# Stored weight sets loaded by quarters, sums reordered, and side work moved in a fused attention and feed-forward kernel

## The chip, the cores and the metric

The kernel runs on one core of a Trainium2 chip. TensorE (PE) multiplies into PSUM; VectorE (DVE) and ScalarE (ACT) read PSUM, convert, add and copy; GpSimd (POOL) does a little; SyncE (SP) issues nearly all the DMAs, from one queue in order. Each engine works through its own queue in order. The metric is the time of one execution on the device in microseconds.

## The reference

```python
scores = 30 * tanh((q @ k.T / 8) / 30)          # 4 batches x 12 heads, 448 x 448, head size 64
attn   = exp(scores - max) / (sum + 1e-9) @ v
x  = attn, heads side by side                    # 1792 tokens x 768
h  = ((x @ w1) * (x @ w2)) @ w3 @ w_out          # 768 -> 1024 -> 1024 -> 768
h  = h @ w_in                                    # 768 -> 1024
s  = h * softmax(h)                              # over 1024
ln = (s - mean(s)) / sqrt(var(s) + 1e-6) * g_ln
out = ln @ moe2_w_out                            # 1024 -> 768
```

## The kernel before

All numbers are float32, and every product is made of float32r matmuls of a high and a low part: three matmuls (high x high, high x low, low x high) for one. A "split" is a cast to the high part on ScalarE or VectorE and a subtraction on VectorE for the low part.

**Attention and fold.** Scores, `tanh`, `exp` and the products with `v` run pair of heads by pair of heads. Between them PE folds `w3 @ w_out @ w_in` into one matrix `w_dr` (DRAM) and starts the gated products. The order is made while the program is built, by a planner (`Order`, `Ahead`) that gives each step a due time from written-out costs. `Ahead` holds a list of tasks (a load into one of three `ld` buffers, a conversion on VectorE, a cast); `plan_w(f)` converts block `f` of `w1` and `w2`, `plan_last(f)` scales block `f` of the output weights by `g_ln` and stores it in `wg_dr`, `plan_x` normalizes the attention's result. A task is loaded and begun in the order of the list.

**Gated products** (`ab`, L1097). Token groups (passes) 0 and 1 are multiplied with all eight blocks of `w1` and `w2`, passes 2 and 3 with two of them, in the plain way. When the attention is over (near 365 us) the rest of the list is emitted two tasks for every 18 matmuls (`fill`, `ahead.step(2)`), and Tile's scheduler orders each engine's queue. In that rest are: `t` sums (`plan_sums("t")`, four subtractions over pieces of `w_dr`, through four `ts` buffers to `tw_dr`), `tg` sums (the same over `wg_dr`, to `tg_dr`), `T` and `U` (sums of the activations, `two_three` and `one_four`), the first weight set and its sums (`first_set`), and the blocks `ws[1]` and `ws[2]` of the folded matrix (`plan_block`), of which `ws[2]` lies in memory that the `U` sums read.

**Seven-product blocks** (`multiply`, L1309). For passes 2 and 3 and the other six blocks n = 0 to 5, seven products of half size stand in for eight: ORDER is 1, 2, 6, 7, 5, 4, 3. Products 1, 2, 7 and 4 take stored weights, 5, 6 and 3 sums of them (`combine`, `combine_low`, `high12`, `low12`). Products 1, 6, 5 and 3 accumulate in one bank `u`, 7 and 4 in a bank `v`; after product index j, `finish(n, j)` copies the bank (`p1s`, `u2s`, `p7s`, ScalarE L1313) or adds it to such a copy (VectorE L1316), and the next product into that bank waits for it. `side[(n, j)]` holds work that is emitted between product j and its `finish`, so that it stands ahead of it in every queue. The weights of set n come from `w12_dr`, and sets n and n + 2 share a place.

**Gated stage** (r = 0 to 6, L1420). Seven products per round with the folded matrix `ws[m]`, then softmax, norm, and rounds 7 to 13 with `wg[m]` in the same way. In round 0 the blocks `ws[5]`, `ws[4]` and `ws[3]` are still being split (`high_w`, ScalarE; `low_w`, VectorE) by `side` entries.

```python
for n in range(AGAIN):
    for j in range(len(ORDER)):
        multiply(n, j)
        for todo in side.pop((n, j), ()):
            todo()
        finish(n, j)
```

Of the kernel before, what the change touches and what calls it, by code (L numbers as in the profile page):

```python
# [241 lines left out]
def attention_moe_solu(ctx: ExitStack, tc: tile.TileContext, q, k, v, cap, w12, w3t, wo, win, wout2, g_ln, out):  # L242
# [422 lines left out]
    plan_o((1, 1))  # L665
    plan_3(0, 6, 7)
    plan_o((2, 0), (3, 0), (2, 1), (3, 1), (4, 0), (4, 1), (5, 0), (5, 1))
    for f in range(3):
        plan_last(f)
    plan_3(1, *range(NF))  # L670
    for f in range(3, 6):
        plan_last(f)
    for c in range(NC):
        plan64(("i", 0, c), win[c, 0], HALF, lambda key=("i", 0, c): slot3(key), reached(passed(1, c - 1) if c else STAGE1 // 2))
    for c in range(NC):
# [258 lines left out]
    plan_w(0)
    plan_x(0)
    plan_w(1)
    plan_x(1)
    for f in range(2, NF):
        plan_w(f)
        if f >= 6:  # L940
            plan_last(f)
    plan_x(2)
    plan_x(3)
    sets, tx, AGAIN = {}, {}, NF - 2
    QUARTER = DM // 2
    AT = {1: (0, 0), 2: (0, 1), 7: (0, 2), 4: (0, 3), 5: (1, 0), 6: (1, 1), 3: (1, 2)}

    def part12(n, m):
        t, at_ = AT[m]
        return sets[n][t][:, :, at_ * QUARTER:(at_ + 1) * QUARTER]  # L950

    def load_set(n):

        if n % 2 == 0:
            sets[n] = [place["set"].tile([P, 2, w * QUARTER], F32R, tag=f"set{w}", name=f"q{w}_{n}") for w in (4, 3)]
        else:
            sets[n] = [res[0].tile([P, 2, 2 * DM], F32R, tag="wres", bufs=2, name=f"q4_{n}")]
        for half in (slice(2 * QUARTER, None), slice(0, 2 * QUARTER)):
            sync.dma_start(out=raw(sets[n][0][:, :, half]), in_=w12_dr[n][:, :, half])

    def set_more(n):
        sets[n].append(res[0].tile([P, 2, 2 * DM], F32R, tag="wres", bufs=2, name=f"q3_{n}"))

    def pieces(n, m):
        t = part12(n, m)
# [18 lines left out]
    def combine_low(n, m):  # L984
        t = whole[n, m]
        b, op_ = (whole.pop((n, m, 0)), ALU.add) if m in (5, 7) else (pieces(n, 1)[1], ALU.subtract) if m == 6 else (pieces(n, 2)[1], ALU.add)
        dve.tensor_tensor(t, t, b, op_)

    def high12(n, m):
        act.copy(part12(n, m)[:, 0], whole[n, m])  # L990
# [3 lines left out]
        dve.tensor_tensor(t[:, 1], whole.pop((n, m)), raw(t[:, 0]), ALU.subtract)  # L994

    def first_set():
        for m in (5, 7, 6):
            combine(0, m)
            combine_low(0, m)
            high12(0, m)  # L1000
        combine(0, 3)
        combine_low(0, 3)
# [11 lines left out]
    def plan_plain(key, do, test, load=lambda: None):  # L1014
        ahead.add(key, load, list, lambda: [("none", 0, 0, 0, do)], None, since(test))
# [13 lines left out]
    def one_four(c):  # L1029
# [10 lines left out]
        dve.tensor_tensor(t, t, l, ALU.add)  # L1040
        split(t4[:, 0], t4[:, 1], t)

    plan_plain("set0", lambda: None, lambda: "set" in place, lambda: load_set(0))
    for i_ in range(NF // 2):
        for part in range(2):
            plan_sums("t", W4, tw_dr, i_, part, HALF // 2)
    for c in range(NC // 2):
        plan_plain(("T", c), lambda c=c: two_three(c), lambda: (NF - 1, 0) in fin)
    for part in range(2):
        plan_block(EARLY[0], part)  # L1050
    for c in range(NC // 2):
        plan_plain(("U", c), lambda c=c: one_four(c), lambda: (NF - 1, 1) in fin)
    plan_plain("first set", first_set, lambda: "set" in place)
    for part in range(2):
        plan_block(EARLY[1], part)
    EARLY_G = 4
    for i_, part in [(i_, part) for i_ in range(NF // 2) for part in range(2)][:EARLY_G]:
        plan_sums("tg", G4, tg_dr, i_, part, DM // 4)
    plan_plain("set1", lambda: None, lambda: (NF, PASSES[1][1]) in fin, lambda: load_set(1))

    def gated_tile(t):
# [5 lines left out]

    begun = {}

    def first_operands():  # L1070
        x1, x2 = lands["x0"], lands["x1"]
        s1, s2 = first_sums = [conv.tile([P, HALF], U32, tag="cv", bufs=2, name=f"s{i}_0").bitcast(F32) for i in (1, 2)]
        begun["sums"] = first_sums

        def begin(m, x):
            begun[m] = w3p.tile([P, 2, HALF], F32R, tag="w3", bufs=W3, name=f"a0_{m}")
            split(begun[m][:, 0], begun[m][:, 1], x)
        begin(1, x1[:, :HALF])
        begin(2, x1[:, HALF:])
        dve.tensor_tensor(s1, x2[:, :HALF], x2[:, HALF:], ALU.add)  # L1080
        dve.tensor_tensor(s2, s1, x1[:, :HALF], ALU.subtract)
        begin(6, s2)
    def gated():
        pp = {}

# [200 lines left out]
        pass  # L1286
    while ahead.step(1):
        pass
    set_more(1)

    side, pu, keeps = {}, {}, {}
    LATER = AGAIN - 1
# [28 lines left out]
    def finish(n, j):  # L1321
        if j in (0, 2, 3):
            keep12(n, *{0: ("u", "p1"), 2: ("u", "u2"), 3: ("v", "p7")}[j])
        elif j == 1:
            plus("y", "p1")
        elif j == 4:
            plus("u", "p7")
        elif j == 5:
            plus("v", "u2")
            dve.tensor_tensor(keeps["u2"], keeps["u2"], keeps["p1"], ALU.mult)  # L1330
            given(n, PASSES[1][0], "u2")
        else:
            dve.tensor_tensor(keeps["p7"], pu["u"], keeps["p7"], ALU.mult)
            given(n, PASSES[1][1], "p7")
# [21 lines left out]
    sums_of = {}

    def tg_load(k):
        landing(f"tg{k}", four(G4, *divmod(k, 2), DM // 4), DM, F32)
        sums_of[k] = []  # L1360

    def tg_half(k, m):
        summed(f"tg{k}", tg_dr, *divmod(k, 2), DM // 4, m, sums_of[k])

    for n in range(AGAIN):
        plan(n, 0, (low12, n, 6), (low12, n, 7), (high12, n, 3))
        plan(n, 1, (low12, n, 5))
        plan(n, 2, (low12, n, 3))
        if n + 1 < AGAIN:
            plan(n, 2, (combine, n + 1, 5))  # L1370
            plan(n, 3, (combine_low, n + 1, 5), (combine, n + 1, 7))
            plan(n, 4, (combine_low, n + 1, 7), (combine, n + 1, 6))
            plan(n, 5, (combine_low, n + 1, 6), (high12, n + 1, 7))
            plan(n, 6, (combine, n + 1, 3), (combine_low, n + 1, 3), (high12, n + 1, 6), (high12, n + 1, 5))
        if n + 2 < AGAIN:
            plan(n, 6, (load_set, n + 2))
            if n % 2:
                plan(n + 1, 0, (set_more, n + 2))
        if n < 2 * NF // 2 - EARLY_G:
            plan(n, 0, (tg_load, EARLY_G + n))  # L1380
            plan(n, 3, (tg_half, EARLY_G + n, 0))
            plan(n, 4, (tg_half, EARLY_G + n, 1))
    plan(LATER - 1, 0, (load_first,))
    plan(LATER, 0, (last_sets,), (load_ws, EARLY[2]), (load_ws, EARLY[3]))
    plan(LATER, 3, (first_operands,))
    plan(LATER, 5, (high_w, ws, EARLY[2], 0), (low_w, ws, EARLY[2], 0))
    plan(LATER, 6, (high_w, ws, EARLY[2], 1), (low_w, ws, EARLY[2], 1), (high_w, ws, EARLY[3], 0))
    with tc.manual_schedule():
# [343 lines left out]
```

## Time and profile before

| | us |
|---|---|
| runs shown: median (lowest to highest) | 794.2 (793.58 to 794.28) |
| profiled execution | 795.62 |
| its span, first to last instruction | 793.8 |
| PE busy in the span | 773.2 |
| VectorE, ScalarE busy | 615.9, 442.2 |

The stages lie in the span so: attention and fold to 365, gated products 270 to 458, six seven-product blocks 458.4 to 550.7, rounds of the gated stage and of the output after that. Times in the rows are from the start of the span. "Busy" counts an instruction from its start to its end; "idle before" is what an engine waited ahead of it, and the releaser is the instruction or DMA whose end let it go.

### The profile page before, as it was taken

Reading aid. Unit: us, or ns where it says so; the run is one execution under the profiler, and the core shown is the slowest. Engines: PE = TensorE matmul, PEld = TensorE weight load, DVE = VectorE, ACT = ScalarE, POOL = GpSimd, SP = SyncE. Lnnn points to the kernel's source line nnn. Section 1 sums busy time; section 2 is a strip of 40 time slices with the busy share of each in tenths; the row PEclk is TensorE's granted clock in tenths of the full one; section 3 lists DMA queues with packets and bytes.
Section 4 is the critical chain, followed back from the end, with each engine's and each line's share of the span. In section 5 each row is a group of like instructions: output and inputs, shape, how many; then the busy total and the mean of one; then the engine's idle time right before and its main releaser. Section 6 shows DMA issues by size and latency. Waiting matters only on the chain.

```text
span 793.8 us, 11282 instructions
## 1 busy us (share of the span) xinstructions
PE 773.2 (97%) x3956; PEld 611.9 (77%) x3956; DVE 615.9 (78%) x1129; ACT 442.2 (56%) x659; POOL 55.1 (7%) x106
## 2 busy tenths in 40 slices
PE   9999999999999999999999959999999999999998
PEld 6556665776866776777999958888688888899998
DVE  6997898989974578865788858787786668878973
ACT  6787867447477766762332212224576666845642
POOL 0111100001010121100000000000011111100000
PEclk9999999999999999999999979999999999999999
DMA  8767868777872484727867884665743335996432
GB/s 282 250 227 235 274 216 293 248 261 247 297 213 79 132 271 142 285 76 294 299 226 251 257 293 165 216 223 173 245 141 123 108 95 132 273 196 134 140 93 80
DMA packets 147672, 162.45 MB, mean 205 GB/s; under 512 B 66148, under 2 KB 116512, under 8 KB 146592
## 3 DMA queue, kind: packets, MB, share of 16 engines
q1 hardware_dynamic: 144880, 155.91, 61.1%
q0 software_dynamic: 2592, 5.73, 3.0%
q8 instruction: 31, 0.51, 0.3%
q14 instruction: 25, 0.20, 0.1%
q10 hardware_dynamic: 144, 0.10, 0.0%
HBM read 114.04 MB, written 47.53 MB: 204 GB/s over the span
## 4 chain that ended last, share of the span: by engine, by line
PE 71%; DMA 11%; DVE 9%; ACT 5%; issue 3%; SPq 1%; DVEq 0%; ACTq 0%
PE u L1420 14%; PE o L523 9%; PE f L775 8%; PE v L1420 7%; PE ab L1097 7%; PE f L759 6%; PE sc L442 6%; PE y L1420 4%; PE us L1309 3%; DMA ldtg<-wg_dr 2%; PE n L523 2%; PE sc L438 2%; DMA ws<-w_dr 2%; DMA wg_dr<-wg 1%; PE vs L1309 1%
## 5 line engine op out<-in xcount | busy, mean ns | idle before, releaser
L1097 PE MATMUL ab<-xs,wt 128*128 128x448 f32 x720 | 148.0, 364 | 0.0
L1097 PEld LDWEIGHTS ab<-xs,wt 128*128 128x128 f32 x720 | 134.3, 188 | 14.4 <-issue 5.2
L455 ACT ACTIVATE sc<-sc,small 128x896 f32<-128x896 f32 (+1 forms) x96 | 82.8, 887 | 46.2 <-PE sc L442 41.4
L460 ACT ACTIVATE p<-sc,small 128x896 f32<-128x896 f32 (+1 forms) x96 | 84.8, 921 | 0.6
L1420 PE MATMUL u<-ws,a 128*128 128x512 f32 x336 | 80.6, 391 | 1.8 <-ACT u L1424 1.3
L523 PE MATMUL o<-p,vd 128*64 128x448 f32 x384 | 77.5, 545 | 0.0
L1420 PEld LDWEIGHTS u<-ws,a 128*128 128x128 f32 x336 | 62.8, 188 | 16.1 <-ACT u L1424 1.8
L759 PE MATMUL f<-w,w_o 128*128 128x512 f32 x288 | 70.8, 396 | 0.0
L775 PE MATMUL f<-w_i,w 128*128 128x512 f32 x288 | 68.6, 393 | 0.0
L759 PEld LDWEIGHTS f<-w,w_o 128*128 128x128 f32 x288 | 53.2, 188 | 16.4 <-issue 3.4
L775 PEld LDWEIGHTS f<-w_i,w 128*128 128x128 f32 x288 | 53.4, 188 | 14.5 <-issue 3.0
L1420 PE MATMUL u<-wg,a 128*128 128x384 f32 x336 | 62.1, 335 | 0.0
L1420 PEld LDWEIGHTS u<-wg,a 128*128 128x128 f32 x336 | 58.5, 188 | 0.5 <-DVE a L1551 0.2
L523 PEld LDWEIGHTS o<-p,vd 128*64 128x64 f32 x384 | 25.4, 136 | 41.2 <-issue 39.9
L331 DVE SCALAR_TENSOR_TENSOR cv<-ld,cv 128x512 uint32<-128x512 uint32 (+1 forms) x80 | 51.7, 659 | 0.8
L334 DVE SCALAR_TENSOR_TENSOR cv<-ld,cv 128x512 uint32<-128x512 uint32 (+1 forms) x80 | 51.8, 660 | 0.7
L1547 ACT CAST a<-s 128x512 fp32r<-128x512 f32 (+1 forms) x42 | 31.3, 754 | 33.4 <-DVE s L1569 16.3
L1551 DVE TENSOR_TENSOR a<-s,a 128x512 fp32r<-128x512 f32 (+1 forms) x42 | 35.5, 852 | 10.2 <-ACT a L1547 10.1
L1420 PE MATMUL v<-ws,a 128*128 128x512 f32 x168 | 40.4, 389 | 0.0
L328 DVE TENSOR_SCALAR cv<-ld 128x512 uint32<-128x512 uint32 (+1 forms) x80 | 32.0, 405 | 10.1 <-ACT wg L652 4.2
L1420 PEld LDWEIGHTS v<-ws,a 128*128 128x128 f32 x168 | 31.5, 188 | 6.6
L481 DVE TENSOR_TENSOR s<-p,p 128x896 f32<-128x896 f32 x18 | 19.6, 1090 | 21.3 <-PE n L523 17.0
(190 smaller groups left out, 1306.2 us busy)
## 6 DMA issues: line engine op xcount, KB each, us to landing
ld<-in_w SPq DMA_DIRECT2D x24, 512.0 KB, 4.9
w_dr<-wt SPq DMA_DIRECT2D x6, 1536.0 KB, 7.8
q<-w_dr SPq DMA_DIRECT2D x12, 768.0 KB, 6.7
ld<-in_w3t SPq DMA_DIRECT2D x16, 512.0 KB, 4.6
w_dr<-e SPq DMA_DIRECT2D x28, 256.0 KB, 3.4
ldx<-ab_dr SPq DMA_DIRECT2D x14, 512.0 KB, 4.3
c_dr<-h SPq DMA_DIRECT2D x14, 512.0 KB, 2.7
ldx<-c_dr SPq DMA_DIRECT2D x56, 128.0 KB, 3.3
```

Of the source, the lines that this page charges most:

```text
L328: dve.tensor_scalar(d[1], d[0][:, :, 1], 5, 2, ALU.logical_shift_left, ALU.logical_shift_right)
L331: dve.scalar_tensor_tensor(d[1], d[0][:, :, 1], 0xC0000000, d[1], ALU.bitwise_and, ALU.bitwise_or)
L334: dve.scalar_tensor_tensor(d[1], d[0][:, :, 0], 29, d[1], ALU.logical_shift_right, ALU.bitwise_or)
L442: pe.matmul(sc[:, j, :S], keys[rows], qq[rows, :], start=(m == 0), stop=(m == len(terms) - 1))
L455: act.activation(sc[:, :w, :S], sc[:, :w, :S], AF.Tanh, scale=qscale)
L460: act.activation(p, sc[:, :w, :S], AF.Exp, scale=capt)
L523: pe.matmul(dst[i * width:(i + 1) * width, :S], weights, moving, start=first, stop=stop)
L759: pe.matmul(banks_[c][0], lw[:, a], fw["3", h, g][:, e], start=begins, stop=(g == NF - 1 and m == 2))
L775: pe.matmul(begun_[m_][0], w34[m_][:, a, c, :], rw[:, e], start=(c == 0 and m == 0), stop=(c == NC - 1 and m == 2))
L1097: pe.matmul(pp[f, b, i][0][:, :S], w[:, u], xs[b, c][:, e], start=begins, stop=(c == NC - 1 and m == 2))
L1420: pe.matmul(banks[g], a[r][m][:, p, k * P:(k + 1) * P], b[m][:, e, k, :], start=(first and k == 0 and i == 0), stop=(k == NF // 2 - 1 and ...
L1551: dve.tensor_tensor(lo, source(r, m), raw(hi), ALU.subtract)
```

## The change

Three parts. **Sets.** A set is no longer loaded as two halves in the last product of a block, but as four quarters in products 1, 2, 4 and 6, each into the place that the block's own products have left; each quarter is now contiguous in a partition. The `tg` sums leave the blocks' side work. **Sums.** The sums of the next set are made in the order 7, 5, 6, 3 (before 5, 7, 6, 3), the last low sum slips into the next block, the low parts of a set are all made in its first two products, and the store of `u2s` goes out one product later. **Order elsewhere.** In the task list, `plan_last(0)` to `(5)` move from among the fold's weights to behind `w(0)`, `w(1)` and `w(5)`; `t` sums stand between `w(5)`, `w(6)` and `w(7)`; `first_set` and then four `tg` sums stand ahead of `T`, the other four ahead of `U`. In block 5 the split of the sixth operand moves from product index 3 to 4, and in round 0 the splits of `ws[5]`, `ws[4]`, `ws[3]` move to later products.

```diff
@@ plan of the fold's weights @@
-    for f in range(3):
-        plan_last(f)
     plan_3(1, *range(NF))
-    for f in range(3, 6):
-        plan_last(f)
@@ task list of the gated products @@
...
-    for f in range(2, NF):
-        plan_w(f)
-        if f >= 6:
-            plan_last(f)
-    plan_x(2)
-    plan_x(3)
...
+    plan_w(0)
+    plan_x(0)
+    for f in range(3):
+        plan_last(f)
+    plan_w(1)
+    plan_x(1)
+    for f in range(3, 5):
+        plan_last(f)
+    for f in range(2, 6):
+        plan_w(f)
+    plan_x(2)
+    plan_x(3)
+    plan_last(5)
     plan_plain("set0", lambda: None, lambda: "set" in place, lambda: load_set(0))
-    for i_ in range(NF // 2):
-        for part in range(2):
-            plan_sums("t", W4, tw_dr, i_, part, HALF // 2)
+    plan_t(0, 1)
+    plan_w(6)
+    plan_last(6)
+    plan_t(2, 3, 4)
+    plan_w(7)
+    plan_last(7)
+    plan_t(5, 6, 7)
+    plan_plain("first set", first_set, lambda: "set" in place and ("x", B - 1, NPAIR // 2 - 1) in xq.done)
+    plan_tg(0, 1, 2, 3)
     for c in range(NC // 2):
         plan_plain(("T", c), lambda c=c: two_three(c), lambda: (NF - 1, 0) in fin)
     for part in range(2):
         plan_block(EARLY[0], part)
+    plan_tg(4, 5, 6, 7)
     for c in range(NC // 2):
         plan_plain(("U", c), lambda c=c: one_four(c), lambda: (NF - 1, 1) in fin)
-    plan_plain("first set", first_set, lambda: "set" in place)
     for part in range(2):
         plan_block(EARLY[1], part)
-    EARLY_G = 4
-    for i_, part in [(i_, part) for i_ in range(NF // 2) for part in range(2)][:EARLY_G]:
-        plan_sums("tg", G4, tg_dr, i_, part, DM // 4)
     plan_plain("set1", lambda: None, lambda: (NF, PASSES[1][1]) in fin, lambda: load_set(1))
@@ sets @@
     def load_set(n):
...
-        for half in (slice(2 * QUARTER, None), slice(0, 2 * QUARTER)):
-            sync.dma_start(out=raw(sets[n][0][:, :, half]), in_=w12_dr[n][:, :, half])
+        open_set(n, 0)
+        if n == 0:
+            open_set(n, 1)
+        for q in (0, 2, 3, 1):
+            load_quarter(n, q)
+    def load_quarter(n, q):
+        sync.dma_start(out=raw(sets[n % 2, 0][:, q]), in_=w12_dr[n][:, :, q * QUARTER:(q + 1) * QUARTER])
     def first_set():
-        for m in (5, 7, 6):
+        for m in (7, 5, 6):
             combine(0, m)
             combine_low(0, m)
+        for m in (7, 5, 6):
             high12(0, m)
@@ side work of the blocks @@
     for n in range(AGAIN):
-        plan(n, 0, (low12, n, 6), (low12, n, 7), (high12, n, 3))
-        plan(n, 1, (low12, n, 5))
-        plan(n, 2, (low12, n, 3))
-        if n + 1 < AGAIN:
-            plan(n, 2, (combine, n + 1, 5))
-            plan(n, 3, (combine_low, n + 1, 5), (combine, n + 1, 7))
-            plan(n, 4, (combine_low, n + 1, 7), (combine, n + 1, 6))
-            plan(n, 5, (combine_low, n + 1, 6), (high12, n + 1, 7))
-            plan(n, 6, (combine, n + 1, 3), (combine_low, n + 1, 3), (high12, n + 1, 6), (high12, n + 1, 5))
-        if n + 2 < AGAIN:
-            plan(n, 6, (load_set, n + 2))
-            if n % 2:
-                plan(n + 1, 0, (set_more, n + 2))
-        if n < 2 * NF // 2 - EARLY_G:
-            plan(n, 0, (tg_load, EARLY_G + n))
-            plan(n, 3, (tg_half, EARLY_G + n, 0))
-            plan(n, 4, (tg_half, EARLY_G + n, 1))
+        follows = n + 1 < AGAIN
+        if n:
+            plan(n, 0, (combine_low, n, 3))
+        plan(n, 0, (low12, n, 6), (high12, n, 3))
+        plan(n, 1, (low12, n, 7), (low12, n, 5), (low12, n, 3))
+        if follows:
+            plan(n, 2, (combine, n + 1, 7))
+            plan(n, 3, (combine_low, n + 1, 7), (combine, n + 1, 5))
+            plan(n, 4, (combine_low, n + 1, 5), (combine, n + 1, 6), (high12, n + 1, 7))
+            plan(n, 5, (combine_low, n + 1, 6), (high12, n + 1, 5))
+            plan(n, 6, (combine, n + 1, 3), (high12, n + 1, 6))
+        if n + 2 < AGAIN:
+            for j, q in ((1, 0), (2, 1), (4, 2), (6, 3)):
+                plan(n, j, (load_quarter, n + 2, q))
+        plan(n, 6, (given, n, PASSES[1][0], "u2"))
...
     plan(LATER, 3, (first_operands,))
+    plan(LATER, 4, (sixth_operand,))
@@ round 0 @@
-    plan(0, 1, (high, 0, 7), (low, 0, 7), (high, 0, 5), (low, 0, 5), (high_w, ws, 5, 0))
-    plan(0, 2, (low_w, ws, 5, 0), (high_w, ws, 5, 1), (high_w, ws, 4, 0))
-    plan(0, 3, (low_w, ws, 5, 1), (high, 0, 4), (sum4, 0), (low_w, ws, 4, 0), (high_w, ws, 4, 1))
-    plan(0, 4, (high, 0, 3), (low, 0, 4), (low_w, ws, 4, 1), (high_w, ws, 3, 0), (high_w, ws, 3, 1))
-    plan(0, 5, (low, 0, 3), (low_w, ws, 3, 0), (low_w, ws, 3, 1))
+    plan(0, 1, (high, 0, 7), (low, 0, 7), (high, 0, 5), (low, 0, 5))
+    plan(0, 3, (high_w, ws, 5, 0), (low_w, ws, 5, 0), (high_w, ws, 5, 1), (low_w, ws, 5, 1), (high, 0, 4), (high_w, ws, 4, 0), (sum4, 0))
+    plan(0, 4, (low, 0, 4), (low_w, ws, 4, 0), (high_w, ws, 4, 1), (low_w, ws, 4, 1), (high, 0, 3), (high_w, ws, 3, 0))
+    plan(0, 5, (low, 0, 3), (low_w, ws, 3, 0), (high_w, ws, 3, 1), (low_w, ws, 3, 1))
```

## Rows read from the trace of the kernel before

**Rows 1.** Part 1 of the page: busy time, share of the span, instructions.

```profile
PE 773.2 (97%) x3956; PEld 611.9 (77%) x3956; DVE 615.9 (78%) x1129; ACT 442.2 (56%) x659; POOL 55.1 (7%) x106
```

**Rows 2.** Windows, PE: blocks 0–5, rounds 0, 1; length, busy, clock, DMA, GB/s.

```profile
458.42:481.57 23.15, 14.96 (x64) 0.78 0.70 251
481.57:495.36 13.79, 13.04 (x64) 1.00 0.62 204
495.36:509.22 13.86, 13.08 (x65) 1.00 0.62 204
509.22:523.77 14.55, 13.16 (x65) 1.00 0.58 195
523.77:536.53 12.76, 12.76 (x65) 1.00 0.78 241
536.53:550.69 14.16, 12.88 (x64) 1.00 0.48 182
550.69:572.20 21.51, 20.02 (x86) 1.00 0.88 266
572.20:591.80 19.60, 19.29 (x86) 1.00 0.30 102
```

**Rows 3.** Waits, 455 to 590: who waited for whom, us, times, longest.

```profile
PE us L1309 <- ACT p1s L1313: 8.2, 1, 8.2
PE us L1309 <- DVE p7s L1316: 2.3, 3, 0.8
PE vs L1309 <- ACT p7s L1313: 1.9, 2, 1.3
PE u L1420 <- ACT u L1424: 1.3, 1, 1.3
```

**Rows 4.** Chain of waits, 455 to 482: start, us, what.

```profile
455.49 6.88 DMA q<-w_dr
462.43 6.34 DMA ws<-w_dr
469.80 0.54 ACT p1s L1313
```

**Rows 5.** Windows: length; busy PE, PEld, DVE, ACT, POOL; clock, DMA, GB/s.

```profile
240.00:260.00 20.00, 20.00 (x108) 12.22 (x107) 8.94 (x14) 14.88 (x23) 1.14 (x2) 1.00 0.23 79
...
372.00:470.40 98.40, 90.21 (x452) 84.06 (x450) 76.88 (x160) 27.96 (x52) 3.50 (x8) 0.97 0.80 267
...
470.40:475.90 5.50, 5.50 (x17) 4.94 (x18) 5.46 (x10) 1.40 (x2) 0.00 (x0) 0.59 0.49 170
```

**Rows 6.** VectorE's groups, 372 to 474: count, busy us, mean ns, idle before.

```profile
L349 DVE TENSOR_TENSOR ws<-ws 128x1024 fp32r<-128x1024 f32 x4 | 4.9, 1224 | 6.0 <-ACT ws L340 6.0
L331 DVE SCALAR_TENSOR_TENSOR cv<-ld,cv 128x384 uint32<-128x384 uint32 x4 | 2.2, 556 | 0.0
L889 DVE TENSOR_TENSOR t<-ld 128x192 f32<-128x192 f32 x4 | 1.4, 356 | 4.1 <-DMA tg_dr<-t 4.1
L892 DVE TENSOR_TENSOR t<-ld 128x192 f32<-128x192 f32 x4 | 1.4, 356 | 3.2 <-DMA tg_dr<-t 2.9 <-DMA tw_dr<-t 0.3
```

**Rows 7.** VectorE's and ScalarE's groups in blocks 1 to 4, 481 to 537.

```profile
L974 DVE TENSOR_TENSOR s<-q 128x384 f32<-128x384 f32 x8 | 4.5, 559 | 5.6 <-DMA q<-w_dr 5.6
L1316 DVE TENSOR_TENSOR p1s<-ys,p1s 128x448 f32<-128x448 f32 x4 | 2.5, 624 | 4.7 <-PE ys L1309 4.7
...
L1313 ACT COPY p7s<-vs 128x448 f32<-128x448 f32 x4 | 2.1, 533 | 10.1 <-DMA ab_dr<-p7s 7.0 <-PE us L1309 3.1
```

**Rows 8.** DMA issues: queue, count, size, median us to landing.

```profile
q<-w_dr SPq DMA_DIRECT2D x12, 768.0 KB, 6.7
ab_dr<-p7s SPq DMA_DIRECT2D x6, 224.0 KB, 6.6
```

**Rows 9.** Timelines of block 5 and of round 0.

```profile
545.87 0.62 ACT L340 CAST a<-s 128x512 fp32r<-128x512 f32 x1 [2.16 <-DVE s L1081]
...
561.22 1.22 DVE L1354 TENSOR_TENSOR ws<-ws 128x1024 fp32r<-128x1024 f32 x1
```

More of the change, by code (lines that the diff above doesn't have):

```diff
@@ L932, in plan_block @@
                   lambda: [("none", 0, 0, 0, lambda: block_split(ws[m], part))], None, there)
[L934 to L937, printed above, removed]
-    for f in range(2, NF):
-        plan_w(f)
-        if f >= 6:
-            plan_last(f)
-    plan_x(2)
-    plan_x(3)
     sets, tx, AGAIN = {}, {}, NF - 2
@@ L949, in part12, with quarters, open_set @@
         t, at_ = AT[m]
-        return sets[n][t][:, :, at_ * QUARTER:(at_ + 1) * QUARTER]
-    def load_set(n):
[L954 to L957, printed above, removed]
-        for half in (slice(2 * QUARTER, None), slice(0, 2 * QUARTER)):
-            sync.dma_start(out=raw(sets[n][0][:, :, half]), in_=w12_dr[n][:, :, half])
-    def set_more(n):
-        sets[n].append(res[0].tile([P, 2, 2 * DM], F32R, tag="wres", bufs=2, name=f"q3_{n}"))
+        return sets[n % 2, t][:, at_]
+    def quarters(t):
+        return t.rearrange("p a n -> p (a n)").rearrange("p (q a n) -> p q a n", a=2, n=QUARTER)
+    def load_quarter(n, q):
+        sync.dma_start(out=raw(sets[n % 2, 0][:, q]), in_=w12_dr[n][:, :, q * QUARTER:(q + 1) * QUARTER])
+    def open_set(n, t):
+        if n == 0:
+            sets[n, t] = place["set"].tile([P, 4 - t, 2, QUARTER], F32R, tag=f"set{t}", name=f"q{t}_{n}")
+        else:
+            sets[n, t] = quarters(res[0].tile([P, 2, 2 * DM], F32R, tag="wres", bufs=2, name=f"q{t}_{n}"))
+    def load_set(n):
+        open_set(n, 0)
+        if n == 0:
+            open_set(n, 1)
+        for q in (0, 2, 3, 1):
+            load_quarter(n, q)
     def pieces(n, m):
@@ L1041, in one_four, with plan_t, plan_tg @@
         split(t4[:, 0], t4[:, 1], t)
-    plan_plain("set0", lambda: None, lambda: "set" in place, lambda: load_set(0))
-    for i_ in range(NF // 2):
-        for part in range(2):
-            plan_sums("t", W4, tw_dr, i_, part, HALF // 2)
+    halves_ = [(i_, part) for i_ in range(NF // 2) for part in range(2)]
+    def plan_t(*items):
+        for k in items:
+            plan_sums("t", W4, tw_dr, *halves_[k], HALF // 2)
+    def plan_tg(*items):
+        for k in items:
+            plan_sums("tg", G4, tg_dr, *halves_[k], DM // 4)
+    plan_w(0)
[11 more added lines that the diff above has]
+    plan_last(5)
+    plan_plain("set0", lambda: None, lambda: "set" in place, lambda: load_set(0))
+    plan_t(0, 1)
[7 more added lines that the diff above has]
+    plan_tg(0, 1, 2, 3)
     for c in range(NC // 2):
@@ L1068, in attention_moe_solu, with begin @@
     begun = {}
+    def begin(m, x):
+        begun[m] = w3p.tile([P, 2, HALF], F32R, tag="w3", bufs=W3, name=f"a0_{m}")
+        split(begun[m][:, 0], begun[m][:, 1], x)
     def first_operands():
@@ L1073, in first_operands @@
         begun["sums"] = first_sums
-        def begin(m, x):
-            begun[m] = w3p.tile([P, 2, HALF], F32R, tag="w3", bufs=W3, name=f"a0_{m}")
-            split(begun[m][:, 0], begun[m][:, 1], x)
         begin(1, x1[:, :HALF])
@@ L1081, in first_operands, with sixth_operand @@
         dve.tensor_tensor(s2, s1, x1[:, :HALF], ALU.subtract)
-        begin(6, s2)
+    def sixth_operand():
+        begin(6, begun["sums"][1])
     def gated():
@@ L1288, in attention_moe_solu @@
         pass
-    set_more(1)
+    open_set(1, 1)
     side, pu, keeps = {}, {}, {}
@@ L1330, in finish @@
             dve.tensor_tensor(keeps["u2"], keeps["u2"], keeps["p1"], ALU.mult)
-            given(n, PASSES[1][0], "u2")
         else:
@@ L1354, in low_w @@
         dve.tensor_tensor(lo, raw(lo), raw(hi), ALU.subtract)
[L1356 to L1363, printed above, removed]
-    for n in range(AGAIN):
-        plan(n, 0, (low12, n, 6), (low12, n, 7), (high12, n, 3))
-        plan(n, 1, (low12, n, 5))
-        plan(n, 2, (low12, n, 3))
-        if n + 1 < AGAIN:
-            plan(n, 2, (combine, n + 1, 5))
-            plan(n, 3, (combine_low, n + 1, 5), (combine, n + 1, 7))
-            plan(n, 4, (combine_low, n + 1, 7), (combine, n + 1, 6))
-            plan(n, 5, (combine_low, n + 1, 6), (high12, n + 1, 7))
-            plan(n, 6, (combine, n + 1, 3), (combine_low, n + 1, 3), (high12, n + 1, 6), (high12, n + 1, 5))
-        if n + 2 < AGAIN:
-            plan(n, 6, (load_set, n + 2))
-            if n % 2:
-                plan(n + 1, 0, (set_more, n + 2))
-        if n < 2 * NF // 2 - EARLY_G:
-            plan(n, 0, (tg_load, EARLY_G + n))
-            plan(n, 3, (tg_half, EARLY_G + n, 0))
-            plan(n, 4, (tg_half, EARLY_G + n, 1))
+    for n in range(AGAIN):
+        follows = n + 1 < AGAIN
[9 more added lines that the diff above has]
+            plan(n, 6, (combine, n + 1, 3), (high12, n + 1, 6))
+        if n + 2 < AGAIN:
+            for j, q in ((1, 0), (2, 1), (4, 2), (6, 3)):
+                plan(n, j, (load_quarter, n + 2, q))
+        plan(n, 6, (given, n, PASSES[1][0], "u2"))
     plan(LATER - 1, 0, (load_first,))
```

## The prediction

> **What bounds the kernel now.** I read the page's busy shares first: TensorE (PE below) is busy 97% of the span [rows 1], so only PE's idle time, and time at a lower clock, can be won; the other engines count only where PE waits for them. The windows by block show where that is [rows 2]. A seven-product block is 63 matmuls. Block 4 is the least disturbed, 12.76 us; block 0 takes 23.15, blocks 1, 2, 3 and 5 take 13.79, 13.86, 14.55 and 14.16. Against block 4 they lose 10.39, 1.03, 1.10, 1.79 and 1.40 us. The first round of the gated stage (r = 0) takes 21.51 us, the next 19.60: 1.91 lost. Together 17.6 us, all of it in code that the diff touches.
>
> The list of waits names the releasers [rows 3]: 8.2 us in one piece for ScalarE's copy `p1s` in block 0, 2.3 us in three pieces for VectorE's addition into `p7s`, 1.9 us in two for ScalarE's copy `p7s`, 1.3 us for the copy of `u` in r = 0. The chain of waits tells what was late in block 0 [rows 4]: half of the second set, on its way for 6.88 us, held SP; then SP issued the load of `ws[2]`, 6.34 us; ScalarE stood at the cast of that load, and the copy `p1s`, next in its queue, came at 469.80. PE was ready for it some 8 us before. `ws[2]` itself is first multiplied in r = 0, after 550. So the stall is queue order: something not urgent, late, ahead of something urgent. It also costs clock: in the 5.5 us after the stall the granted clock is 0.59 [rows 5], 5.5 x 0.41 = 2.3 us, contained in the 10.39.
>
> Behind that chain stands VectorE. From 372 to 470.4 it is busy 76.88 us of 98.4 [rows 5], so 21.5 us idle; 6.0 of these wait for casts of `ws`, 7.3 for stores of sums to leave the four `ts` buffers (4.1 and 3.2) [rows 6].
>
> **The change part by part.** I sum against the profiled execution, 795.62 us (span 793.8 and 1.8 around it); the median of the runs shown, 794.2, is 1.42 lower.
>
> *Scaled output weights (`plan_last` 0 to 4)* move from early in the attention to behind `w(0)` and `w(1)`. Ten halves, each three VectorE passes of at most 0.556 us [rows 6], 16.7 us at most; VectorE is busy 8.94 of 20 us in 240 to 260 [rows 5], and PE is fully busy there. Cost 0, hidden by those 11 us of idle time and the like around them; without them it would be the 16.7 at the very most. I allow 1 us either way for the planner's other order.
>
> *The drain before block 0.* `plan_last(5)` now stands behind `w(5)`, and all eight `tg` sums instead of four are made here. VectorE gets 4 x 4 x 0.356 = 5.7 us for the sums and 2 x 3 x 0.556 = 3.3 for the weights [rows 6]: 76.9 + 9.0 = 85.9 us from 372 on, and its tail ends at 372 + 85.9 + W, with W its idle time (21.5 before). What shrinks W: five `t` sums stand ahead of `w(7)`, the first set ahead of the `T` and `U` sums, so there is ready work where VectorE waited for `ws` (6.0), and the last stores are spread over a longer time (I take half of 7.3, 3.7). W = 21.5 - 6.0 - 3.7 = 11.8, tail at 469.7. Behind the tail VectorE's own order in block 0 is the addition `p1s`, seven sums of the next set, the addition `p7s`: 0.62 + 7 x 0.559 + 0.62 = 5.1 us [rows 7], so 474.8. PE's seventh product needs that at 458.42 + 10.8 = 469.2. Loss in block 0: 5.6 us, in general W - 6.2. Bounds: nothing (W under 6.2, ScalarE's cast behind the urgent copies), or all of the 10.39. What else is moved: four more `tg` bring 16 more DMAs to SP's queue before block 0 and out of the blocks, the second set is four loads instead of two, and whatever SP waits for there holds the stores of `abs` and the load of `ws[2]`.
>
> *Blocks 1 to 4.* Before, set n comes as two 768 KB loads issued in the last product of block n - 2, three products ahead of the first sum that reads it; the sums wait for it, and the store of `p7s` queues behind it and lands 6.6 us after issue [rows 8]; so ScalarE's `p7s` copy waits 7.0 us in total for the buffer [rows 7]. After, quarters start in products 1, 2, 4 and 6 of block n - 2, each as PE leaves its place; by the walk below the last has some 7.6 us before the sum that reads it, the others 10 and more, where a half landed in 6.7 [rows 8]. My walk, with 0.56 us for a VectorE operation, 0.62 for an addition from PSUM, 0.53 for a copy [rows 7], 0.25 from the end of a product to its reader, and products ending each 1.8 us from the block's start: the last multiplication of the block before ends at 0.9; low sum 3 and the low parts 6, 7, 5, 3 at 3.7 (6 at 2.0, needed at 3.6; 7 at 2.6, needed at 5.4); `p1s` at 4.5; both sums 7, low 7, both sums 5, low 5 and sum 6 at 8.4; `p7s` waits for its product and is done at 9.9, needed at 10.8; the rest ends at 13.5, 0.9 into the next block. Every step has 0.9 us or more to spare. ScalarE's copy at 7.45 needs the store of the last `p7s`, issued at about 1.2 behind one 384 KB quarter instead of 1.5 MB: it must land within 6.2 us. The `tg` sums (1.4 us a block) are gone. I put blocks 1 to 3 at block 4's time: 1.03 + 1.10 + 1.79 = 3.9 us gained; at least half of it, should the store be late.
>
> The Trainium skill speaks against small transfers: "DMA: Bandwidth & Descriptors", Rules for kernel authors, wants at least 1 MiB a DMA for the full rate, and its fit in the section on the anatomy of one DMA (measured on GpSimd's path) would give a 384 KB quarter 2.9 us and a 768 KB half 3.8, an estimate: 11.6 us a set in place of 7.6 if one came after the other. Were the sums as late by that, the 3.9 us would be lost, 788.7. No row here shows a quarter. By the rows the quarters need not be faster than the halves were, and I keep the 3.9.
>
> *Block 5.* ScalarE's third cast, which waits 2.16 us for VectorE [rows 9], moves behind the copy `p7s`, so the 1.3 us stall at product 5 (the longest of that kind in [rows 3]) goes. The addition `p7s` is late next: the cast starts at 545.87 and takes 0.62, the low part behind it and the addition some 0.62 each, 547.7; needed at 536.53 + 10.8 = 547.3. With the hand-overs 0.5 of the 1.40 stays: 0.9 gained (bounds 0 and 1.4).
>
> *r = 0.* The casts of `ws[5]` and `ws[4]` that held the copy of `u` move behind it, so that wait (1.3) [rows 3] goes. But VectorE's subtractions set the pace: the first starts at 561.22 [rows 9], and it now waits for a cast pushed back by the copy, about 0.2 us. The later ones are the same number. I take +0.2 (bounds: 1.3 gained, 1 lost).
>
> **Sum.** 10.39 - 5.6 = 4.8; 3.9; 0.9; less 0.2: 9.4 us. 795.62 - 9.4 = 786.2 profiled, 784.8 as median.
>
> **Rivals.**
> *Clean* (0.14): W falls under 6.2 and block 0 is undisturbed: 5.6 more, 779.2. For it: tasks not urgent have 30 us of slack. Against: VectorE would have to be busy over 93% from 372 on.
> *The stall stays* (0.21): its chain (set, then `ws[2]`, then cast) does not run through the sums. The load of `ws[2]` still stands behind `U` and the set's loads, now four, and the cast still stands in one queue with the copies. Block 0 keeps its 10.4: 789.6.
> *Slower, the tail overflows* (0.15): the added transfers are 4.3 MB (four `tg` in and out, 3.1; weights 5, 1.2), and the stretch moved 267 GB/s [rows 5]; at that rate they are 16 us. If no wait shrinks and a quarter of that shows, W is 25.5, the loss in block 0 is 19.3, 799 as median. It decides at W - 6.2 = 10.39 + 4.6, W = 21.2: about the idle time of before.
> *The store of `p7s` stays late* (0.07): should it still take 6.6 us [rows 8], the copy starts at 7.8 + 0.3, product 5 has nothing to spare, and VectorE's `p7s` comes late as before: about 3 us of the 3.9 are not won, 787.8. The page's rule on small transfers points this way.
>
> **How the numbers follow.** The forecast has 0.43 (loss in block 0 of 2 to 8 us: 781 to 787.5). The range, 777.5 to 793, takes in the clean case with 1.5 us for r = 0 and the staying stall with 3 us more; it leaves out the overflow and the tails, under 2 in 10. A measurement of this kernel tells about 0.2% (1.6 us) from no change. All but the overflow end faster by more than that; with a part of the overflow near W = 21: faster 0.80, same 0.05, slower 0.15.
>
> **What would show it.** Right: blocks 1 to 4 within 0.3 us of 12.76, no waits of VectorE for the set's load, no wait of ScalarE for the store of `p7s`; block 0 between 13 and 20 us with a clock above 0.9; block 5 near 13.3; r = 0 near 21.7. Wrong: a block 0 above 23 us, or idle PE before 458 (at `w(7)`, whose conversion now stands behind three more sums), or blocks 1 to 3 above 13.5.

## The result, and the profile after

The changed kernel takes 802.8 us (median of four runs, 801.1 to 805.9), the kernel before 794.2 (793.6 to 794.4). The ratio is 1.0114, 95% interval 1.0078 to 1.0150: slower by 1.1%, where 784.8 and faster was forecast. The profiled execution of the changed kernel is the slowest of its four, 805.94 us with a span of 804.2; the one of before had 795.62 and 793.8. So the two traces differ by 10.4 us, the medians by 8.6.

The waits of TensorE (PE) come first: the page's first part, and the list of waits (who waited for whom, us, times, longest).

```profile
PE 778.8 (97%) x3956; PEld 617.6 (77%) x3956; DVE 617.6 (77%) x1134; ACT 440.8 (55%) x654; POOL 54.4 (7%) x106
```

```profile
PE ab L1120 <- ACT wt L340: 9.8, 2, 7.2
PE us L1332 <- ACT u2s L1336: 3.9, 1, 3.9
PE sc L438 <- ACT p L460: 3.0, 2, 2.3
...
PE u L1432 <- DVE ws L1376: 0.9, 2, 0.5
...
PE v L1432 <- DVE ws L1376: 0.5, 1, 0.5
...
PE us L1332 <- DVE p7s L1339: 0.3, 1, 0.3
```

Against [rows 3], the 2.3 us for `p7s`, the 1.9 for the copy `p7s` and the 1.3 for the copy of `u` are gone or nearly; the stall in block 0 is 3.9 us, not 8.2, and has a later copy as its end. New are 9.8 us ahead of the blocks, in the products `ab`, for casts of stored weights (`wt`), and 3.0 in the attention. The windows by stage, TensorE (length, busy, granted clock, DMA share, GB/s), first the products `ab`, two stretches of them, then blocks 0 to 5 and rounds 0 and 1:

```profile
369.87:477.42 107.55, 97.44 (x464) 0.94 0.83 275
400.00:420.00 20.00, 17.14 (x77) 0.91 0.66 230
420.00:440.00 20.00, 12.76 (x52) 0.74 0.88 304
477.42:497.04 19.62, 15.71 (x64) 0.83 0.83 265
497.04:509.64 12.60, 12.60 (x64) 1.00 0.53 160
509.64:522.24 12.60, 12.60 (x64) 1.00 0.51 161
522.24:534.84 12.60, 12.60 (x64) 1.00 0.56 163
534.84:547.44 12.60, 12.60 (x64) 1.00 0.49 149
547.44:560.63 13.19, 12.88 (x64) 1.00 0.51 196
560.63:582.10 21.47, 20.07 (x85) 1.00 0.88 266
582.10:601.70 19.60, 19.30 (x86) 1.00 0.29 97
```

The same stretch of `ab` products in the kernel before, which had no idle time:

```profile
365.13:458.42 93.29, 93.29 (x467) 1.00 0.78 260
```

The account of the 10.4 us: the attention ends at 369.87 in place of 365.13, +4.7; the `ab` products +14.3 (10.1 idle, 4.2 more busy time at a lower granted clock, 0.94); block 0 from 23.15 to 19.62, -3.5; blocks 1 to 4 from 54.96 together to 50.40, -4.6; block 5 -1.0; round 0 -0.04; what comes after round 1 +0.5. The blocks won 9 us, and what the diff did to the task list ahead of them cost 19.

Where the 9.8 us come from is in the chain of waits (start, us, what), in SP's timeline, which shows when loads were issued, and in TensorE's timeline (idle before in brackets):

```profile
398.25 11.38 DMA ld<-in_w
...
422.87 5.83 DMA ld<-in_w
428.80 0.44 DVE cv L328
```

```profile
406.80 2.99 SPq L318 DMA_DIRECT2D ld<-in_wout  x2
...
412.57 7.60 SPq L316 DMA_DIRECT2D ld<-w_dr  x4
...
420.91 1.17 SPq L316 DMA_DIRECT2D ld<-w_dr  x2
...
422.87 0.37 SPq L318 DMA_DIRECT2D ld<-in_w  x1
```

```profile
407.48 1.08 PE L1120 MATMUL ab<-xs,wt 128*128 128x448 f32 x4 [2.54 <-ACT wt L340]
...
431.59 4.85 PE L1120 MATMUL ab<-xs,wt 128*128 128x448 f32 x12 [7.25 <-ACT wt L340]
```

The `ld<-in_wout` pair is `plan_last(6)`, the `ld<-w_dr` loads are the three `t` sums that `plan_w(7)` now stands behind. The first of weight block 7's three loads is issued at 422.87; its conversion starts on VectorE at 428.80, the cast follows, and TensorE, which had stood still for 7.25 us, goes on at 431.59. In the kernel before the last of the three had been issued by 401.07:

```profile
394.95 1.81 SPq L318 DMA_DIRECT2D ld<-in_w  x2
...
401.07 0.33 SPq L318 DMA_DIRECT2D ld<-in_w  x1
```

### The profile page after: what moved, and what is told of

Same layout as the page of the kernel before. It is cut to its first block, busy times and chain, and to the rows that moved or that the text cites. A ratio compares the mean times of both kernels' runs of the same rounds, so it can differ in the third digit from the quotient of the medians.

```text
span 804.2 us, 11305 instructions
## 1 busy us (share of the span) xinstructions
PE 778.8 (97%) x3956; PEld 617.6 (77%) x3956; DVE 617.6 (77%) x1134; ACT 440.8 (55%) x654; POOL 54.4 (7%) x106
## 4 chain that ended last, share of the span: by engine, by line
PE 74%; DMA 10%; DVE 8%; ACT 4%; issue 3%; SPq 0%; POOL 0%; DVEq 0%; ACTq 0%; POOLq 0%
PE u L1432 14%; PE ab L1120 8%; PE f L755 8%; PE o L523 7%; PE f L771 7%; PE v L1432 7%; PE sc L442 5%; PE us L1332 5%; PE y L1432 4%; DMA ld<-in_w 3%; PE vs L1332 2%; PE n L523 2%; PE sc L438 2%; DMA rb<-r_dr 2%; DMA tg_dr<-t 1%
## 5 line engine op out<-in xcount | busy, mean ns | idle before, releaser
L1120 PE MATMUL ab<-xs,wt 128*128 128x448 f32 x720 | 154.8, 374 | 10.1 <-ACT wt L340 9.8
L1120 PEld LDWEIGHTS ab<-xs,wt 128*128 128x128 f32 x720 | 138.7, 194 | 26.6 <-ACT wt L340 10.5
L328 DVE TENSOR_SCALAR cv<-ld 128x512 uint32<-128x512 uint32 (+1 forms) x80 | 32.2, 406 | 14.1 <-DMA ld<-in_w 7.9
```

The source lines that it names most:

```text
L1120: pe.matmul(pp[f, b, i][0][:, :S], w[:, u], xs[b, c][:, e], start=begins, stop=(c == NC - 1 and m == 2))
```

## The experiments

Eleven kernels, each beside fresh runs of the kernel before (794.1 to 794.4 in all groups); the table's first row repeats the result. "The drain" is the part of the task list that runs beside the `ab` products, from the end of the attention to block 0. "Waits" are TensorE's idle us for casts of `wt`, from each kernel's list of waits.

| run | time, us | ratio to before, 95% | waits |
|---|---|---|---|
| the change | 802.8 | 1.0114 [1.0078, 1.0150] | 9.8 |
| weights 6, 7 before set and `t` | 788.0 | 0.9927 [0.9903, 0.9951] | 0 |
| weights 6, 7 before `t` alone | 789.6 | 0.9930 [0.9902, 0.9957] | 0 |
| scaled weights 0 to 5 early | 792.6 | 0.9976 [0.9961, 0.9991] | 6.2 |
| scaled weights 0 to 4 early | 795.2 | 1.0018 [0.9995, 1.0040] | 10.8 |
| before, weights 6, 7 late | 797.4 | 1.0050 [1.0034, 1.0067] | 5.2 |
| both orders put right | 787.7 | 0.9923 [0.9903, 0.9942] | 0 |
| the same, `ws[2]` in the blocks | 785.7 | 0.9899 [0.9881, 0.9918] | 0 |
| old task list, new blocks | 787.8 | 0.9917 [0.9894, 0.9941] | 0 |
| the same, `ws[2]` in the blocks | 783.1 | 0.9866 [0.9844, 0.9888] | 0 |
| the same, three `tg` in the drain | 781.4 | 0.9827 [0.9801, 0.9853] | 0 |
| before, `ws[2]` in the blocks | 790.7 | 0.9958 [0.9941, 0.9975] | 0 |

**Is it the weight blocks?** Weight blocks 6 and 7 ahead of the set and all `t` sums:

```
+    plan_w(6); plan_last(6); plan_w(7); plan_last(7)
     plan_plain("set0", ...)
-    plan_t(0, 1); plan_w(6); plan_last(6); plan_t(2, 3, 4); plan_w(7); plan_last(7); plan_t(5, 6, 7)
+    plan_t(*range(8))
```

> The changed kernel with one edit: in the task list, the weight blocks 6 and 7 and the scaled output weights 6 and 7 stand ahead of the first set's load and of all eight t sums. Theory (landing buffers): the gated products of the changed kernel take 107.5 us instead of 93.3 because the loads of blocks 6 and 7 wait for the three landing buffers that the t sums in front of them hold; with the edit PE waits under 1 us for casts of wt and the gated products take 93 to 95 us. The t sums then all come late, so block 0 loses more than the 7 us it loses now, 10 to 16. Time 793 to 798. Rival (too much work in the drain): the four tg sums and the scaled block 5 that were added fill VectorE and the DMA engines, so blocks 6 and 7 are late in any order; PE still waits 8 us or more for wt, time 800 to 803.

Measured 788.0, 15 us under the change: no wait for `wt`, the `ab` products take 368.67 to 461.34, 92.7 us. The theory was right about the loads and wrong about the time, its range began 5 us higher: the later `t` sums do not cost block 0 the 10 to 16 us that it gave them. The waits of the attention stay, and some 4 us in blocks 0 and 1:

```profile
PE sc L438 <- ACT p L460: 2.8, 2, 2.4
PE vs L1330 <- ACT p7s L1334: 2.6, 1, 2.6
PE us L1330 <- ACT u2s L1334: 1.4, 1, 1.4
```

The order of these loads alone undoes the 14.3 us of the `ab` products, and with them more than the 8.6 us by which the change is slower.

**The `t` sums or the set?** The same, but the set's four loads stay ahead of the two weight blocks.

```
     plan_plain("set0", ...)
-    plan_t(0, 1); plan_w(6); plan_last(6); plan_t(2, 3, 4); plan_w(7); plan_last(7); plan_t(5, 6, 7)
+    plan_w(6); plan_last(6); plan_w(7); plan_last(7); plan_t(*range(8))
```

> The change with one edit: weight blocks 6 and 7 and their scaled halves stand ahead of all t sums, but still behind the loads of the second set; scaled weights late, as in the change. Theory (the t sums in the three landing buffers are what held the two weight blocks): no wait for their casts before block 0, as in the run that also moved them ahead of the set, 787 to 789. Rival (the set's four loads, which wait for their place at the end of the attention, hold SP's queue and so the weights): a wait of 2 us or more for the casts remains, 791 to 797.

Measured 789.6 (786.1 to 791.5), 0.6 above the theory's range, and no wait for `wt`. It is the `t` sums, not the set. No run changed the number of landing buffers or the pace at which the list is emitted, so which of the two made the loads behind the `t` sums late is not separated.

**What do the late scaled weights add?** Weights 0 to 5 scaled in the attention again, the rest as in the change:

```
     plan_3(0, 6, 7) ...
+    for f in range(3): plan_last(f)
     plan_3(1, *range(NF))
+    for f in range(3, 6): plan_last(f)
...
-    for f in range(3): plan_last(f)        # behind w(0)
-    for f in range(3, 5): plan_last(f)     # behind w(1)
-    plan_last(5)                           # behind w(5)
```

> The changed kernel with one edit: the scaled output weights 0 to 5 stand again among the fold's weights in the early attention. Theory: the attention of the changed kernel ends 4.7 us later (PE waits 3.0 us for exponentials and runs 1 to 2 us at a lower clock) because ten scaled halves now compete with the attention between 200 and 260 us; with the edit the attention ends near 365 and the drain has one scaled block less, so the time falls by 4.7 to 7, to 796 to 798. Rival (the planner's order falls out otherwise by chance, whatever is moved): the attention still waits 2 us or more somewhere, time 800 to 803.

Measured 792.6, 10.2 us under the change and 3.4 below the range that the theory gave: it counted the attention and at most 2.3 us more. The attention ends at 365.28, so the 4.7 us lost there in the change came from the moved scaled weights. In the change the longest of those waits was at 316.61: the copies and `p` of ScalarE stood, in queue order, behind a cast that waited 4.39 us for VectorE's `many` (ScalarE's and VectorE's timelines of the change):

```profile
312.82 0.56 ACT L340 CAST xs<-many 128x448 fp32r<-128x448 f32 x1 [4.39 <-DVE many L843]
...
315.55 1.90 ACT L460 ACTIVATE p<-sc,small 128x896 f32<-128x896 f32 x2
```

```profile
311.64 1.15 DVE L843 SCALAR_TENSOR_TENSOR many<-many,xs,rb 128x896 f32<-128x896 f32 x1 [2.15 <-DMA rb<-r_dr]
```

Of the 9.8 us for `wt` 6.2 stay. Then the same with only 0 to 4 early; the two halves of block 5 stay behind `w(5)`:

```
+    for f in range(3): plan_last(f)
     plan_3(1, *range(NF))
+    for f in range(3, 5): plan_last(f)
...
-    for f in range(3): plan_last(f)        # behind w(0)
-    for f in range(3, 5): plan_last(f)     # behind w(1)
```

> The change with the scaled weights 0 to 4 back early in the attention; only those of weight block 5 stay late, behind weight block 5 itself. It tells why the late scaled weights and the late weight blocks together cost more than each alone (waits for casts: 9.8 us in the change, 6.2 with scaled weights 0 to 5 early). Theory A (block 5's two loads and stores in the landing buffers push weight block 7 back): waits of some 9 to 10 us for the casts, 796 to 800, though the attention ends at 365 to 366. Theory B (the attention's delay of 4.7 us is carried into the drain by work that follows it): waits of 6 to 7 us, 792 to 794, as with all six early.

Measured 795.2, and theory A held for the wait: block 7's first load is issued at 416.38 where it was at 412.20 with all six early (SP's timelines of the two runs, this one and then the one before it), and TensorE waits 10.31 us in place of 6.19.

```profile
416.38 0.38 SPq L318 DMA_DIRECT2D ld<-in_w  x1
```

```profile
412.20 0.38 SPq L318 DMA_DIRECT2D ld<-in_w  x1
```

The time is 1 us under the range given for A. In the traces the `ab` products take 5.2 us longer than with all six early (107.47 for 102.26); of that the attention, which ends 1.2 us earlier (364.10), and block 0 (14.4 for 14.9) give some back.

**The late weights alone.** The kernel before, with the places that the change gives to weight blocks 6 and 7:

```
-    for f in range(2, NF): ... (with plan_last for f >= 6)
+    for f in range(2, 6): plan_w(f)
...
+    plan_t(0, 1); plan_w(6); plan_last(6); plan_t(2, 3, 4); plan_w(7); plan_last(7); plan_t(5, 6, 7)
```

> The kernel before with one edit: weight block 6 and its scaled halves stand behind the second set and two t sums, weight block 7 and its halves behind three more t sums, as in the change; all else as before. Theory (this order alone starves TensorE ahead of block 0): waits for the casts of weights of some 10 us and a lower clock, 10 to 14 us slower than before less what a later block 0 finds ready, 800 to 808. Rival: it takes the scaled weights' delay in the attention too, or the quarters' four loads in place of two, to make the wait: under 3 us slower, 794 to 797.

Measured 797.4 (794.1 to 798.9), 3.3 us slower than before: less than the theory said, more than the rival did. The traced execution is the fastest of the seven, 794.09, with a span of 792.3 against 793.8 before, so it shows the wait but not the 3.3 us. The wait is 5.2 us for one cast, and the `ab` matmuls take 150.6 us of busy time against 148.0, so 7.8 us are lost ahead of block 0. But the stall of block 0 shrinks from 8.2 us to 1.3:

```profile
PE ab L1105 <- ACT wt L340: 5.2, 1, 5.2
...
PE us L1317 <- ACT p1s L1321: 1.3, 1, 1.3
```

Block 0 itself takes 14.1 us (466.10 to 480.24) for 23.15. The chain to `ws[2]` ends when it ends; in this execution the time that TensorE lost ahead of block 0 came back in block 0. Where the slower six lost their time no trace shows.

**Both orders put right.** The first and the third edit together:

> The change with both orders of the task list put right: scaled weights 0 to 5 early in the attention, weight blocks 6 and 7 (and their scaled halves) ahead of the second set and of all t sums. Theory, two separate costs (4.7 us in the attention from the scaled weights, the rest from the two weight blocks that stand behind sums): both go, attention ends at 365 to 366, no wait for the casts of weights before block 0, and the time is 788.0 less some 3.5, 784 to 785. Rival: VectorE's work is only pushed on, into the drain, and block 0 takes back what the attention gains: 787 to 789, with block 0 at 23 us again.

Measured 787.7, the rival's time, where the scaled weights late gave 788.0. The attention's waits are 0.8 us, the `ab` products end at 458.2, and block 0, 21.4 us long, stands still at its third product (TensorE's and ScalarE's timelines):

```profile
467.64 3.73 PE L1329 MATMUL us<-t,q 128*128 128x448 f32 x9 [5.70 <-ACT p1s L1333]
```

```profile
464.85 1.04 ACT L340 CAST ws<-ws 128x1024 fp32r<-128x1024 f32 x1 [8.48 <-DMA ws<-w_dr]
...
467.06 0.53 ACT L1333 COPY p1s<-us 128x448 f32<-128x448 f32 x1
```

It is the stall of [rows 4] again: the copy stands behind casts of `ws[2]`, which nothing needs yet. What the attention gained waited there.

**The blocks without the new task list.** The change's blocks, quarters and round 0 with the task list of before, four `tg` sums in the drain and four in the blocks:

```
-    (the change's list from plan_w(0) to the second block of ws)
+    (the list of before, EARLY_G = 4)
+        if n < 2 * NF // 2 - EARLY_G:
+            plan(n, 0, (tg_load, EARLY_G + n))
+            plan(n, 3, (tg_half, EARLY_G + n, 0)); plan(n, 4, (tg_half, EARLY_G + n, 1))
```

> The changed kernel with the whole task list of the kernel before (scaled weights, t sums, first set, four tg sums in the drain and four in the blocks); what stays of the change are the quarters, the order of the sums in the blocks, the later split of the sixth operand and the order in round 0. Theory (the sets' loads and the store behind them delay the blocks): blocks 1 to 4 take 12.6 to 12.8 us with the tg sums in them, block 5 13.2, block 0 loses 10 as in the kernel before: 794.2 - 5.5 = 788.7. Rival (the blocks of the changed kernel are clean because the tg sums left them): blocks 1 to 3 stay at 13.2 us or more, time 791 to 793.

Measured 787.8, 6.4 us under before and 0.9 under the theory's 788.7. Blocks 1 to 4 take 12.60 us each even with a `tg` sum in each; block 0 waits 5.84 us behind the casts of `ws[2]`. So the blocks and round 0 win their 6 us without the new task list.

**The stall of block 0.** The load of `ws[2]` moved from the drain to block 1, its casts and subtractions to blocks 2 and 3, in four kernels:

```
-    for part in range(2): plan_block(EARLY[1], part)
+    plan(1, 0, (load_second,))
+    for i in range(2):
+        plan(2 + i, 5, (high_w, ws, EARLY[1], i))
+        plan(2 + i, 6, (low_w, ws, EARLY[1], i))
```

In the kernel before:

> The kernel before with one edit: the load of ws[2] and its two splits leave the drain; the load is issued in block 1, the splits stand in products 5 and 6 of blocks 2 and 3. Theory (queue order: ScalarE's copies stand behind a cast that waits for this load): block 0 takes 12.8 to 15 us instead of 23.15, the clock stays full, blocks 2 and 3 lose up to 0.5 us more; time 784 to 786.5. Rival (VectorE's tail of sums is the real limit and only hidden by the cast): PE waits in block 0 for VectorE's additions instead, 4 to 6 us lost, time 788 to 791.

Measured 790.7, the rival's time and not the theory's: the wait for `p1s` is gone, and VectorE's `abs`, 3.76 us, is late next. With both orders put right:

> As the run with both orders put right, and the load of the second sum of weights moved from the drain to block 1, its casts to blocks 2 and 3. Theory: block 0 still waits for ScalarE's cast of that load, so the stall of 4 to 6 us and its clock go: 3 to 5 us under the other run of this pair, 780 to 782. Rival: VectorE's tail, which makes all eight G4 sums before block 0, is as late as the cast, and block 0 stays where it is: within 1.5 us of the other run, with the wait now named for VectorE.

Measured 785.7, 2.0 us gained, between the two: the casts are gone, but VectorE, with all eight `tg` sums in the drain, still makes them between block 0's own sums. TensorE waits 2.84 us for the copy `p7s`; the profile names VectorE's sum `s7l` as what released that copy, and ahead of that sum VectorE had waited several times for stores of `tg` (ScalarE's and VectorE's timelines):

```profile
470.54 0.53 ACT L1331 COPY p7s<-vs 128x448 f32<-128x448 f32 x1 [4.38 <-DVE s7l L972]
```

```profile
466.04 0.36 DVE L892 TENSOR_TENSOR t<-ld 128x192 f32<-128x192 f32 x1 [1.79 <-DMA tg_dr<-t]
```

With the old task list, so four `tg` sums in the drain:

> The change's blocks, quarters and first gated round with the whole task list of before, so four G4 sums in the drain and four in the blocks (787.8 us without the next edit), and the load of the second sum of weights moved to block 1, its casts to blocks 2 and 3. Theory: the 5.8 us wait for the copy behind the cast goes and VectorE's tail, some 3 to 4 us, is what is left: 784 to 786. Rival: the blocks, now with sums, casts and loads together, lose what block 0 gains: 787 to 789, with blocks 2 and 3 above 13 us.

Measured 783.1, 1 us below the theory's range. And with three:

```
-    EARLY_G = 4
+    EARLY_G = 3
```

> The fastest version so far (the change's blocks and first gated round, before's task list, the second sum of weights loaded and cast in the blocks; 783.1 us) with three G4 sums made before block 0 in place of four, and five in the blocks. There block 0 still waits 1.05 us for VectorE's sums abs and 0.94 for its addition p7s. Theory: VectorE's tail is 1.4 us shorter, both waits go or shrink, 781 to 782.5. Rival: the waits are set by the copies' and products' own order, or block 4 loses with a sum what block 0 gains: 782.8 to 785.

Measured 781.4, 1.7% under the kernel before and the fastest here; 1.8 us separate it from the version with four, and the intervals of the two ratios overlap slightly. The wait for `p7s` in block 0 is gone, the one for `abs` stays, 1.10 us. Block 0 takes 457.47 to 471.84, 14.4 us (TensorE's timeline; the last line holds block 0's seventh product and block 1's first):

```profile
457.47 1.96 PE L1325 MATMUL us<-xs,q 128*128 128x448 f32 x9
...
464.14 2.08 PE L1325 MATMUL vs<-t,q 128*128 128x448 f32 x9 [1.10 <-DVE abs L1132]
...
469.93 3.88 PE L1325 MATMUL us<-xs,q 128*128 128x448 f32 x18
```

## Why the prediction was wrong

**The failed step: the drain before block 0.** It summed VectorE's work from 372 on and its idle time, and let the result show only in block 0, with TensorE at block 0's start at 458.42 as before. Nothing in it asked when weight blocks 6 and 7 would be loaded. They are TensorE's own operands before 458; the list puts them behind five `t` sums and block 5's scaled weights, all through the same landing buffers, and block 7's first load leaves at 422.87, when before all three had left by 401.07. That cost 14.3 us in the stretch that the prediction took as full, of which 10.1 were idle. The sign was named at the end (idle PE before 458 at `w(7)`) and priced at nothing: the five sums were counted as "ready work", a gain of 6.0 us in W. Put ahead of the `t` sums, the two blocks give the time back (788.0). The edit on the kernel before and the run with the fifth scaled weight alone show two parts of the wait that add up: the `t` sums, 5 to 6 us, and what else is put in ahead, 4.1 us more for two halves of scaled weights.

**Scaled weights at cost 0: wrong.** The price was read from VectorE's share and TensorE's full busy share in 240 to 260 [rows 5]. The term was 0, with 1 us either way; the attention lost 4.7 us, 2.7 of it idle, the rest at a lower granted clock (0.93 in 300 to 320). At 316 it is the order in ScalarE's queue that stands behind the wait. The early placement takes the loss away. How the planner came to that other order was not followed further.

**Block 0: half right.** Lost 6.9 us against block 4's 12.76 where 5.6 were forecast, but not by VectorE's additions, and that the sizes are near is luck. W did not shrink to 11.8: from 372 to the addition `p1s` at 484.69 VectorE was busy 84.64 of 112.69 us, so 28 idle, and TensorE came 19 us later. The rival "the stall stays" named the wait: the cast at 487.17 waits 7.16 us for `ws<-w_dr`, and the copy `u2s` stands behind it. VectorE's sums come in ahead of that: SP issued the load right behind three stores of `tg` sums (ScalarE's and SP's timelines; the window has busy PE, PEld, DVE, ACT, POOL).

```profile
487.17 1.04 ACT L340 CAST ws<-ws 128x1024 fp32r<-128x1024 f32 x1 [7.16 <-DMA ws<-w_dr]
488.12 0.53 ACT L1336 COPY u2s<-us 128x448 f32<-128x448 f32 x1
```

```profile
479.60 1.53 SPq L890 DMA_DIRECT2D tg_dr<-t  x3
481.23 1.28 SPq L914 DMA_DIRECT2D ws<-w_dr  x2
```

```profile
372.00:484.69 112.69, 102.58 (x489) 94.41 (x487) 84.64 (x182) 29.52 (x53) 3.41 (x8) 0.94 0.84 273
```

That the stall is shorter fits TensorE coming to the block 19 us later, as in the run of before with the late weights, where it shrank to 1.3. Both runs that kept the load in the drain and came to block 0 on time, near 458, stood there for 5.7 and 5.8 us, and taking the load out of the drain gave 2.0 to 4.7 us.

**Blocks 1 to 4: right**, 4.6 us for 3.9: each block 12.60 us, 0.16 under the least disturbed block of before, which was the yardstick. VectorE's sums of the set wait for no load, and ScalarE's `p7s` copy for no store (groups of 497 to 547):

```profile
L967 DVE TENSOR_TENSOR s<-q 128x384 f32<-128x384 f32 x8 | 4.4, 550 | 0.0
...
L1336 ACT COPY p7s<-vs 128x448 f32<-128x448 f32 x4 | 2.1, 532 | 5.1 <-PE vs L1332 5.1
```

A quarter lands in 3.8 us where a half took 6.7 [rows 8]; issued as places come free, no sum waits for one. The Trainium skill ("DMA: Bandwidth & Descriptors", Rules for kernel authors) asks for at least 1 MiB a DMA for the full rate, which speaks against the split. The fit in its section on the anatomy of one DMA (measured on GpSimd's path, where these loads are issued by SP) gives 2.9 us for a quarter and 3.8 for a half, an estimate; both measured times are longer, and the gain came all the same.

```profile
q<-w_dr SPq DMA_DIRECT2D x24, 384.0 KB, 3.8
```

**Block 5: right** (1.0 for 0.9). **Round 0: right in size**: 21.47 for 21.51, 0.2 worse forecast; VectorE's subtractions (0.9 and 0.5 us) took the place of the wait for ScalarE's copy, as argued.

The sum without the failed steps would have been -3.5, -4.6, -1.0: 9.1 us, near the 9.4 forecast; the two steps ahead of it were +4.7 and +14.3. The rival on the slower side, 799, had the sign and was 4 us off in the time, but it had the wrong place: it put an overflow of VectorE's tail into block 0.

## What to carry to other kernels

When a diff reorders a task list, walk each buffer ring and queue that the list feeds, and ask of every load that is passed when its consumer on the bound engine needs it; a full engine's share of 97% holds only as long as its operands keep coming. A stall behind a late chain can absorb time lost ahead of it and swallow time gained there: two gains in a row are worth what the later stall allows, so remove the last stall first. Work that isn't needed yet (here the load and casts of `ws[2]`, and the `tg` sums) is best put where the queues have room: moved into the blocks, it gave 6.5 us together, and the blocks still took 12.6.

## What was not expected of the hardware

A 512 KB load of weights that the chain follows took 11.38 us from its issue at 398.25, where the median of such loads in this kernel is 4.5; the DMA share in 400 to 420 was 0.66, and what it queued behind was not tried. Quarters took longer in the versions with `tg` sums in the blocks: 3.8 us in the change, 4.3 with the old task list, 4.7 in the fastest version, where the DMA share of blocks 1 to 4 was about 0.5, 0.7 and 0.8. That the traffic is the cause was not tried; blocks 1 to 4 took 12.60 us in all three.

```profile
q<-w_dr SPq DMA_DIRECT2D x24, 384.0 KB, 4.3
```

```profile
q<-w_dr SPq DMA_DIRECT2D x24, 384.0 KB, 4.7
```
